# A new order for the prologue of a sketched-attention and expert-routing kernel

## The chip, the cores and the metric

The kernel runs on one core of one Trainium2 chip. A core has a matmul engine (TensorE; PE in the profile, with its weight loads listed as PEld), three engines for elementwise work (VectorE, ScalarE and GpSimd; DVE, ACT and POOL in the profile) and DMA queues, which the SyncE engine (SP) and others issue to. Every engine works through its own instructions in the order of the program, and waits for others by semaphores. Matmul operands lie in SBUF, results land in PSUM, which is divided into banks.

The metric is the device time of the whole program in microseconds, taken as a median over runs. All inputs start in DRAM and the output ends there.

## The reference

Two blocks follow each other. The first is attention with a polynomial sketch instead of a softmax: each row of q and k (32 numbers) is turned into 64 features, the outer product of two projections to 8 numbers.

```python
# q, k, v: (4, 4, 1088, 32) float32; S1, S2: (8, 32), float64
def phi(x):
    a = np.einsum('rd,bhsd->bhsr', S1, x)
    b = np.einsum('rd,bhsd->bhsr', S2, x)
    return np.einsum('bhsi,bhsj->bhsij', a, b).reshape(*x.shape[:-1], 64)
q_p, k_p = (phi(q), phi(k))
kv = np.einsum('bhsf,bhsd->bhfd', k_p, v)
z = np.sum(k_p, axis=2)
num = np.einsum('bhsf,bhfd->bhsd', q_p, kv)
den = np.einsum('bhsf,bhf->bhs', q_p, z)[..., None] + 1e-06
attn_out = (num / den).astype(np.float32)
```

The second block takes the result as 4352 rows of 128 and sends each row to one of 8 experts by a hash of its token number.

```python
x = attn_out.transpose(0, 2, 1, 3).reshape(4352, 128)
expert_idx = token_ids * np.int64(2654435761) % np.int64(8)
for e in range(8):                      # w1: (8, 128, 1024), w2: (8, 1024, 128)
    mask = expert_idx == e
    h = np.maximum(x[mask] @ w1[e], 0.0)
    out[mask] = h @ w2[e]
```

## The kernel before

*Stages.* The program has a prologue, four attention batches and an expert stage. The order of the instructions on each engine is written out by hand; nothing is reordered by a scheduler, so the order of the source is the order of each engine's queue.

*Rows of a batch.* The 1088 rows of a batch are 1024 main rows (8 tiles of 128 partitions, called T, handled as two groups g of Q = 4) and 64 tail rows, which are handled for two batches together. Work on a tile always covers the 4 heads.

*Attention, one batch b.* PE transposes k (`turned`, L458 on) and ACT copies the result to SBUF (`kT`, L470). PE multiplies it with the sketch matrix `s_k`, both projections at once (`k_products`, L499, matmul at L496), which gives 16 numbers per row and head in PSUM. ACT copies all of them to SBUF (`ab`, L511). DVE multiplies the two halves into 64 features (`kp`, L523, two operations per batch, one for each group). PE sums `kv` over the rows (`kv_products`, matmul at L554) from the features and `va`, which is v with a column of ones. For q, DVE makes the transpose (`qT`, L590, and L730 for the first batch), PE the products (`q_products`, `abq_ps`), ACT the copy, DVE the features (`f`, L523) and their transpose (`fT`, L606). ACT cuts the blocks of `kv` that belong to each head into `m` (L576), 16 small copies, whose other entries were zeroed at the start (L229). PE multiplies `fT` with `m` into `x_ps` (L658), ACT copies to `xe` (L661), and DVE (`den`) and GpSimd (`xs`, L686) divide. A store then writes the rows to `x_rows` in DRAM. In the loop each batch also prepares the k and q features of the next one.

*Sketch matrix.* S1 and S2 are 64-bit floats[...]. DVE takes them apart as integers and puts the 32-bit value together (L242 to L266, `s_rep`). One PE transpose and one DVE product with a mask turn this into `s_k` (`s_turned`, L273).

*Routing.* Beside attention, DVE and GpSimd sort the tokens by expert: `route_experts` and `route_scan` count, `route_counts` has three matmuls and an ACT copy (`counts`), `route_bases` finds each expert's place (L323 to L339), `route_order` and `route_ranks` follow, then `route_digits` and `route_slots` on GpSimd and `route_rows`/`route_tiles` on DVE (L416, L426).

*PSUM.* Three pools: `ps` with 4 banks (`bank()`), `ps_x` with 2 (`x_bank`), `ps_o` with 2 (kv sums; later the second layer's sums).

*Loads.* SP issues the loads of all batches (L119), in an order written out at L150 to L161; two tensors of the first batch, and k with them, come in two halves each. ACT's queue brings S2 and the token numbers. The experts' weights follow on SP's queue as soon as the order of the experts is known.

*PE at the start.* Ten matmuls without a result (`keep_busy(WARM)`, L210) run before the first real work, and one more between the k transposes and the first products.

*Expert stage.* Sixteen groups (two for each expert) run through layer 1 (`hp`, L943) and layer 2 (`op`, L951), interleaved. Rows are gathered by GpSimd with indirect DMAs, and result rows are scattered to the output by GpSimd too (L954). GpSimd's queue holds two drains, placed after step 7 of groups 12 and 14 (L1063)[...]. At the end of the stage the last results (`op_rows`, L1140) are copied by ACT (L1142) and scattered.

Of the kernel before, what the change touches and what calls it, by code (L numbers as in the profile page):

```python
# [9 lines left out]
F32 = mybir.dt.float32  # L10
# [20 lines left out]
def kernel(  # L31
# [42 lines left out]
    WARM = 10  # L74
# [25 lines left out]
    nc.scalar.dma_start(tok[:], _words(moe_token_ids).rearrange("(p c two) -> p c two", p=P, two=2))  # L100
# [12 lines left out]
    def load_main(src, b, tag):  # L113
        t = load.tile([P, H, T, D], F32, tag=tag, name=f"{tag}{b}")
        n = parts(b, tag)
        for g in range(n):
            nc.sync.dma_start(t[:, :, g * T // n:(g + 1) * T // n],
                              src[b, :, g * SM // n:(g + 1) * SM // n, :].rearrange("h (p t) d -> p h t d", t=T // n))
        return t  # L119

    def parts(b, tag="q"):

        return 2 if b == 0 else 1
# [25 lines left out]

    act = const.tile([P, 1], F32)  # L150
    nc.scalar.memzero(act[:])
    k_t += [load_main(k, b, "k") for b in range(2)]
    v_t.append(load_main(v, 0, "v"))
    q_t.append(load_main(q, 0, "q"))
    k_tail = load_tail(k, "k_tail")
    v_tail = load_tail(v, "v_tail")
    q_t.append(load_main(q, 1, "q"))
# [70 lines left out]
    for m in ms[0] + ms[1]:  # L228
        nc.scalar.memzero(m[:])  # L229
# [16 lines left out]
    m_hi = shifts("m_hi", hi, 12, 9)  # L246
    nc.vector.tensor_scalar(ex[:], ex[:], 127.0 - 1023.0, 0.0, op0=OP.add, op1=OP.max)
    m_lo = s_tile("m_lo")
    nc.vector.tensor_scalar(m_lo[:], lo, 29, None, op0=OP.logical_shift_right)
    nc.vector.tensor_scalar(ex[:], ex[:], 255.0, None, op0=OP.min)  # L250
    sg = s_tile("sg")
    nc.vector.tensor_scalar(sg[:], hi, 31, 31, op0=OP.logical_shift_right, op1=OP.logical_shift_left)
    live = s_tile("live", F32)
    nc.vector.tensor_scalar(live[:], ex[:], 0.0, None, op0=OP.is_gt)
    nc.vector.tensor_scalar(ex[:], ex[:], 23, None, op0=OP.logical_shift_left)
    rest = shifts("rest", lo, 3, 3)
    nc.vector.tensor_tensor(sg[:], sg[:], ex[:], op=OP.bitwise_or)
    s32 = s_tile("s32", F32)
    nc.vector.tensor_copy(s32[:], rest[:])
    top = s_tile("top")  # L260
    nc.vector.tensor_tensor(top[:], m_hi[:], m_lo[:], op=OP.bitwise_or)
# [193 lines left out]

    x_dram = nc.dram_tensor("x_rows", (N, DM), F32)

    def turned(src, g):  # L458

        p = bank([P, H, P], "kT_ps")  # L460
        for h in range(H):
# [782 lines left out]
```

## Time and profile before

| what | value |
|---|---|
| median of 3 runs | 193.56 us (193.52 to 193.78) |
| profiled execution | 190.24 us |
| its span (first to last recorded instruction) | 188.4 us |
| first kv sum of batches 0, 1, 2, 3 starts | 9.43, 26.94, 39.71, 50.76 us |
| first matmul of the expert stage | 62.33 us |
| end of the last matmul | 183.6 us |

All times inside the program are us from the start of the span. A line of the timeline gives start, duration, engine, source line, operation, output and inputs by the program's names, shapes, the number of instructions it stands for, and in brackets how long the engine was idle before it and what released it. In the table by stage a pair such as "3.93 (x10)" is busy time and number of instructions of one engine.

Some durations that are used below, from the groups by shape up to the start of the expert stage:

| instruction | mean |
|---|---|
| DVE `kp`, 128x1024 (x8) | 1.439 us |
| DVE `f`, 128x1024 (x8) | 1.263 us |
| DVE `fT`, 128x1024 (x8) | 1.246 us |
| DVE `qT`, 128x1024 (x3) / 128x512 (x2) | 1.223 / 0.686 us |
| DVE `kp_tail`, 128x512 | 0.649 us |
| DVE `row` (x2) / `in_tile` / `tiles` | 1.268 / 0.789 / 0.796 us |
| ACT `m` from `kv`, 32x66 (x48) | 0.206 us |
| ACT `xe`, 128x264 | 0.38 us |

### The profile page before, as it was taken

The page shows a single profiled execution, that of the slowest core. Times are in us where ns is not written, and L with a number is a line of the kernel's source. Part 1 is how long each engine was busy: PE and PEld are TensorE (multiplying, and loading weights), DVE is VectorE, ACT ScalarE, POOL GpSimd, SP SyncE. Part 2 cuts the span into 40 slices and gives each one's busy share as a digit, 9 for nine tenths or more (in the row PEclk, how much of TensorE's full clock was granted, in tenths as well). Part 3 has the DMA queues.
Part 4 walks back from the last instruction along what each step waited for, and adds up shares of the span by engine and source line. Part 5 has one row for each costly group of instructions (what it writes and reads, how often), then busy time and mean ns, then how long its engine had stood idle before and what let it go on. Part 6 is the DMA issues. An engine that isn't in the chain of part 4 may idle for free.

```text
span 188.4 us, 3334 instructions
## 1 busy us (share of the span) xinstructions
PE 180.0 (96%) x1066; PEld 154.1 (82%) x1066; DVE 112.3 (60%) x304; ACT 72.9 (39%) x227; POOL 108.1 (57%) x153
## 2 busy tenths in 40 slices
PE   7979999999999999989999999999999999999990
PEld 2869999999998888878888888777777777778990
DVE  5899997999979747455346345345254754424330
ACT  6733783776527432233232232232331323311320
POOL 7258983737482558756766467463664434244573
PEclk9999999999999999999999999999999999999999
DMA  4999999989395721623443343431614243060011
GB/s 125 302 191 294 349 355 342 338 251 339 131 251 153 247 70 44 171 63 84 98 82 77 83 84 66 89 84 42 92 50 95 48 95 69 14 99 28 27 47 36
DMA packets 40115, 25.91 MB, mean 138 GB/s; under 512 B 21236, under 2 KB 37301, under 8 KB 40096
## 3 DMA queue, kind: packets, MB, share of 16 engines
q1 hardware_dynamic: 35152, 18.46, 37.3%
q0 software_dynamic: 2416, 5.08, 10.8%
q10 hardware_dynamic: 2528, 2.13, 4.0%
q8 instruction: 9, 0.15, 0.3%
q14 instruction: 10, 0.08, 0.1%
HBM read 17.41 MB, written 4.52 MB: 116 GB/s over the span
## 4 chain that ended last, share of the span: by engine, by line
PE 72%; DVE 15%; POOL 7%; issue 3%; ACT 1%; POOLq 0%; DVEq 0%
PE hp L943 31%; PE op L951 31%; DVE kp L523 4%; PE kv L554 3%; DVE f L523 3%; PE idle L210 2%; POOL out_dram L954 2%; DVE fT L606 2%; PE ab_ps L496 1%; DVE row L416 1%; PE x_ps L658 1%; PE abq_ps L496 1%; POOL va L541 1%; DVE m L576 1%; POOL over L403 1%
## 5 line engine op out<-in xcount | busy, mean ns | idle before, releaser
L951 PE MATMUL op<-hT,w 128*128 128x256 f32 (+8 forms) x256 | 76.3, 389 | 0.0
L811 DVE TENSOR_SCALAR hT<-hp 128x256 f32<-128x256 f32 (+9 forms) x68 | 29.0, 427 | 54.1 <-PE hp L943 44.8
L954 POOL DMA_INDIRECT out_dram<-os,put x35 | 35.7, 1019 | 38.4 <-DVE os L1012 21.3
L951 PEld LDWEIGHTS op<-hT,w 128*128 128x128 f32 x256 | 47.4, 190 | 10.6
L809 ACT ACTIVATE hT<-hp 128x256 f32<-128x256 f32 (+9 forms) x68 | 26.5, 390 | 64.6 <-PE hp L943 64.1
L803 POOL DMA_INDIRECT xg<-x_rows,idx x33 | 33.9, 1028 | 18.7 <-DVE idx L863 5.6
L943 PE MATMUL hp<-xT_late,w 128*128 128x320 f32 (+8 forms) x144 | 41.9, 386 | 0.0
L943 PE MATMUL hp<-xT,w 128*128 128x256 f32 x128 | 37.1, 380 | 0.5 <-ACT half L991 0.5
L943 PEld LDWEIGHTS hp<-xT_late,w 128*128 128x128 f32 x144 | 25.4, 190 | 6.8
L943 PEld LDWEIGHTS hp<-xT,w 128*128 128x128 f32 x128 | 24.1, 190 | 4.1 <-ACT half L991 0.9
L554 PE MATMUL kv<-va,kp 128*128 128x132 f32 x128 | 15.7, 278 | 0.5 <-DVE kp L523 0.3
L658 PE MATMUL x_ps<-m,fT 128*128 128x132 f32 x128 | 15.7, 279 | 0.1
L554 PEld LDWEIGHTS kv<-va,kp 128*128 128x128 f32 x128 | 14.8, 190 | 0.9 <-issue 0.9
L658 PEld LDWEIGHTS x_ps<-m,fT 128*128 128x128 f32 x128 | 14.9, 190 | 0.4 <-ACT xe L661 0.3
L576 ACT COPY m<-kv 32x66 f32<-32x66 f32 x48 | 9.9, 206 | 7.0 <-PE kv L554 6.4
L686 POOL TENSOR_TENSOR xs<-xe,den 128x512 f32<-128x512 f32 x6 | 7.7, 1302 | 7.7 <-DVE den L681 4.1
L523 DVE TENSOR_TENSOR kp<-ab 128x1024 f32<-128x1024 f32 x8 | 11.2, 1439 | 0.6 <-ACT ab L511 0.6
L1012 DVE COPY os<-turned 128x256 uint16<-128x256 uint16 (+1 forms) x26 | 7.5, 312 | 5.0 <-DMA turned<-half 4.7
L606 DVE STREAM_TRANSPOSE fT<-f 128x1024 f32<-128x1024 f32 x8 | 10.0, 1246 | 0.5
L523 DVE TENSOR_TENSOR f<-ab 128x1024 f32<-128x1024 f32 x8 | 10.1, 1263 | 0.1
L882 DVE COPY xh<-xg 128x256 uint16<-128x256 uint16 (+1 forms) x28 | 9.5, 380 | 0.0
L496 PE MATMUL abq_ps<-s_k,qT 128*128 128x128 f32 (+1 forms) x64 | 7.8, 274 | 1.4 <-DVE qT L730 1.4
(196 smaller groups left out, 175.7 us busy)
## 6 DMA issues: line engine op xcount, KB each, us to landing
w<-in_moe_w_dram SPq DMA_DIRECT2D x12, 512.0 KB, 6.9
w<-in_moe_w_dram ACTq DMA_DIRECT2D x4, 512.0 KB, 5.1
k<-in_k_dram SPq DMA_DIRECT2D x3, 512.0 KB, 7.5
q<-in_q_dram SPq DMA_DIRECT2D x3, 512.0 KB
v<-in_v_dram SPq DMA_DIRECT2D x3, 512.0 KB, 8.6
x_rows<-xs SPq DMA_DIRECT2D x2, 512.0 KB, 3.2
out_dram<-os,put POOLq DMA_INDIRECT x35, 2.3
xg<-x_rows,idx POOLq DMA_INDIRECT x33, 2.6
```

The source lines that it names most:

```text
L496: nc.tensor.matmul(dst, stationary, s.rearrange("p t x r -> p t (x r)").unsqueeze(1).to_broadcast([s.shape[0], n, s.shape[1], 2 * R]), sta ...
L523: eng.tensor_tensor(dst, ab[:, :, 0].unsqueeze(3).to_broadcast(shape), ab[:, :, 1].unsqueeze(2).to_broadcast(shape), op=OP.mult)
L554: nc.tensor.matmul(kv[:].rearrange("p x y -> p (x y)")[:, pr * HA:(pr + 1) * HA], kp[:, t, 2 * pr:2 * pr + 2].rearrange("p h i j -> p (h i ...
L576: copy(m[f][t * D:(t + 1) * D, h::2, t], src)
L606: nc.vector.transpose(fT[:].rearrange("p k (q s) -> p k q s", q=Q), f[:].rearrange("p q h (k d) -> p (h k) q d", d=D))
L658: nc.tensor.matmul(p[:, h], fT[:, (h0 + h) * FB + fb], m[fb][:, h0 + h].rearrange("p t d -> p (t d)"), start=(fb == 0), stop=(fb == FB - 1 ...
L803: nc.gpsimd.indirect_dma_start(out=dst, out_offset=None, in_=x_dram[0:rows], in_offset=bass.IndirectOffsetOnAxis(ap=idx, axis=0), bounds_c ...
L809: nc.scalar.activation(dst, src, AF.Relu if relu else AF.Copy)
L811: return nc.vector.tensor_scalar(dst, src, 0.0, None, op0=OP.max).ins
L943: nc.tensor.matmul(hp[:, 0:hi - lo], w1[:, g % E, c * P:(c + 1) * P], x_columns(first_of(g) + lo, first_of(g) + hi), start=True, stop=True)
L951: nc.tensor.matmul(ops[g][:, 0:hi - lo], w2[:, g % E, c], hTs[g][:, c, lo:hi], start=(c == 0), stop=(c == FC - 1))
L954: st_ = nc.gpsimd.indirect_dma_start(out=out[:], out_offset=bass.IndirectOffsetOnAxis(ap=idx, axis=0), in_=src, in_offset=None, bounds_che ...
```

## The change

The diff touches the prologue and the first turns of the loop, the way features are formed in all batches, two PSUM banks in the last batch, and one drain near the end:

- *Start.* 6 instead of 10 matmuls without a result, and the extra one is gone. The 64-bit to 32-bit conversion has 9 DVE operations instead of 16. Zeroing `m` moves: the first pair to DVE, the second to a later point on ACT.
- *Loads.* k of the first batch comes in four pieces of 128 KB, one of them on ACT's queue, with the token load behind it; v and q of the first batch come whole; q of the second batch is loaded ahead of `v_tail`. The rows of the first batch are stored to `x_rows` with one DMA instead of two.
- *First k.* The sketch's transpose comes first on PE, k is transposed in pairs of heads with an ACT copy each.
- *Features.* ACT copies only the first factor (`first_copied`). DVE reads the second factor from PSUM (`features_of`). The tails keep both factors in SBUF. A products bank is therefore in use until DVE has formed the features; k products are put into `kv_bank`, some others into `x_bank`.
- *Order.* Transposes and products of the second k come ahead of the first kv sum, which then runs in two parts (steps 0 and 1, then all others). `route_bases` is split into `route_places` and the rest, with q's transposes between. In the first turn of the loop the kv tail and the first-factor copy of q come ahead of q's tail products, the tail features ahead of `kp`. `row1`, `in_tile` and `tiles` come after the second `f`.
- *Last batch.* `bring(0)` takes a `kv_bank`, the last x products a `bank`.
- *Drain.* The second drain moves from the end of group 14's step 7 to its step 0.

The core of the diff:

```diff
-    WARM = 10
+    WARM = 6
...
+        for i, eng in enumerate((nc.sync, nc.scalar, nc.sync, nc.sync)):
+            ts, hs = slice(i // 2 * Q, (i // 2 + 1) * Q), slice(i % 2 * 2, (i % 2 + 1) * 2)
+            eng.dma_start(t[:, hs, ts], rows[:, hs, ts])
...
+    k_t.append(load_main(k, 0, "k"))
+    load_tok()
     act = const.tile([P, 1], F32)
     nc.scalar.memzero(act[:])
-    k_t += [load_main(k, b, "k") for b in range(2)]
+    k_t.append(load_main(k, 1, "k"))
     v_t.append(load_main(v, 0, "v"))
     q_t.append(load_main(q, 0, "q"))
     k_tail = load_tail(k, "k_tail")
+    q_t.append(load_main(q, 1, "q"))
     v_tail = load_tail(v, "v_tail")
-    q_t.append(load_main(q, 1, "q"))
...
-    for m in ms[0] + ms[1]:
-        nc.scalar.memzero(m[:])
+    for m in ms[0]:
+        nc.vector.memset(m[:], 0.0)
...
-    m_hi = shifts("m_hi", hi, 12, 9)
-    nc.vector.tensor_scalar(ex[:], ex[:], 127.0 - 1023.0, 0.0, op0=OP.add, op1=OP.max)
...
-    nc.vector.tensor_add(s32[:], s32[:], top[:].bitcast(F32))
+    sign = s_tile("sign")
+    nc.vector.tensor_scalar(sign[:], hi, -(1 << 31), 1 << 30, op0=OP.bitwise_and, op1=OP.bitwise_xor)
+    nc.vector.tensor_scalar(ex[:], ex[:], 1023.0 + 128.0, 1023.0 - 127.0, op0=OP.min, op1=OP.max)
+    high = s_tile("high")
+    nc.vector.tensor_scalar(high[:], hi, (1 << 20) - 1, 1 << 20, op0=OP.bitwise_and, op1=OP.bitwise_or)
+    nc.vector.tensor_scalar(ex[:], ex[:], 24, 1, op0=OP.logical_shift_left, op1=OP.logical_shift_right)
+    low = s_tile("low")
+    nc.vector.tensor_scalar(low[:], lo, 1, None, op0=OP.logical_shift_right)
+    nc.vector.tensor_tensor(ex[:], ex[:], sign[:], op=OP.bitwise_xor)
     s32 = s_tile("s32", F32)
+    nc.vector.scalar_tensor_tensor(s32[:], low[:], 2.0 ** -31, high[:], op0=OP.mult, op1=OP.add)
     s_rep = const.tile([2 * R, Q, D], F32)
+    nc.vector.scalar_tensor_tensor(s_rep[:], s32[:].unsqueeze(1).to_broadcast([2 * R, Q, D]), 2.0 ** -20,
+                                   ex[:].bitcast(F32).unsqueeze(1).to_broadcast([2 * R, Q, D]), op0=OP.mult, op1=OP.mult)
...
+    def pair_turned(kT, src, g, pr):
+        hs = slice(2 * pr, 2 * pr + 2)
+        nc.scalar.copy(kT[:, hs], turned(src, g, range(H)[hs])[:])
...
+    def first_copied(ab_ps):
+
+        n = ab_ps.shape[1] * H * Q
+        a = work.tile([P, n, R], F32, tag="first", name="first_of_ab", bufs=3)
+        nc.scalar.copy(a[:], ab_ps[:].rearrange("p g t h y -> p (g t h) y")[:, :, 0:R])
+        return a, ab_ps[:].rearrange("p g t h y -> p (g t h) y")
+
+    def features_of(dst, ab, g):
+
+        a, ps_ = ab
+        r = slice(g * H * Q, (g + 1) * H * Q)
+        shape = [P, H * Q, R, R]
+        nc.vector.tensor_tensor(dst, a[:, r].unsqueeze(3).to_broadcast(shape),
+                                ps_[:, r, R:2 * R].unsqueeze(2).to_broadcast(shape), op=OP.mult)
...
+    kTs = [kT_tile() for _ in range(GQ)]
+    s_turned(x_bank)
+    pair_turned(kTs[0], k_t[0], 0, 0)
+    pair_turned(kTs[0], k_t[0], 0, 1)
+    pair_turned(kTs[1], k_t[0], Q, 0)
     route_experts()
-    kTs = [transposed(k_t[0], 0)]
-    s_turned()
-    kTs.append(transposed(k_t[0], Q))
-    keep_busy(1)
     route_scan()
     va = values(v_t[0], T, work, "", None)
-    abk = ab_tile()
     kp = work.tile([P, T, H, R, R], F32, tag="kp", name="kp", bufs=1)
-    parts_ps = [k_products(kTs[g:g + 1]) for g in range(GQ)]
-    copy_ab(abk, parts_ps[0], 0, src=0)
+    abks = [first_copied(k_products(kTs[0:1], kv_bank))]
     nc.scalar.copy(cp[:], seq[:, :, C - 1])
-    copy_ab(abk, parts_ps[1], Q, src=0)
-    k_features_of(kp, abk, 0, Q)
+    pair_turned(kTs[1], k_t[0], Q, 1)
+    abks.append(first_copied(k_products(kTs[1:2], x_bank)))
+    for g in range(GQ):
+        k_features_main(kp, abks[g], g, 0)
+    kTs = [transposed(k_t[1], g) for g in range(0, T, Q)]
     cnt = route_counts()
+    abk_ps = k_products(kTs, kv_bank)
     for g in range(GQ):
         ts = slice(g * Q, (g + 1) * Q)
         nc.scalar.copy(va[:, ts, :, 0:D], v_t[0][:, :, ts].rearrange("p h t d -> p t h d"))
-    kTs = [transposed(k_t[1], g) for g in range(0, T, Q)]
-    kv = kv_products(0, (kp, va), (kp_tail, va_tails), None, upto=Q)
-    k_features_of(kp, abk, Q, T)
-    route_bases(cnt)
+    abk = first_copied(abk_ps)
+    route_places(cnt)
     route_order()
...
+    kv = kv_products(0, (kp, va), (kp_tail, va_tails), None, upto=2)
     kTt = k_tail_turned()
+    abqs = [first_copied(q_products(qT[:, :, 0:Q], Q, x_bank))]
+    abt = k_tail_products(kTt)
+    abqs.append(first_copied(q_products(qT[:, :, Q:T], Q, x_bank)))
+    route_bases(cnt)
+    for m in ms[1]:
+        nc.scalar.memzero(m[:])
     digits = route_ranks()
     route_order_end()
...
-    kv = kv_products(0, (kp, va), (kp_tail, va_tails), kv, Q + 2)
     route_digits(digits)
-    abt = k_tail_products(kTt)
-    abk_ps = k_products(kTs)
     kv = kv_products(0, (kp, va), (kp_tail, va_tails), kv, T)
-    abk = copied(abk_ps)
-    fTs = [q_features(abq, 0)]
     k_features_of(kp_tail, abt, 0, TT)
     qT = q_blocks(q_t[1], T)
     qT_tail = q_tail_blocks()
-    fTs.append(q_features(abq, 1))
+    fTs = [q_features(abqs[0], 0, 0)]
+    fTs.append(q_features(abqs[1], 1, 0))
...
         m = kv_diagonal(b, kv)
         if b == 0:
-            tail = q_tail_copied(abt_ps)
+            m_tail = kv_tail(b, kv)
+            abq = first_copied(abq_ps)
+            tail = q_tail_copied(q_tail_products(qT_tail))
             kT_ps = [turned(k_t[b + 2], g) for g in range(0, T, Q)]
+            fT_tail = q_tail_features(tail)
         else:
-            abk = copied(abk_ps)
+            abk = first_copied(abk_ps)
         kp = k_features(abk, T, work, "")
...
-    bring(0)
-    x_products(e, 1, fTs[1], last_m)
+    bring(0, kv_bank)
+    x_products(e, 1, fTs[1], last_m, bank)
...
-        if g in (G - 4, G - 2):
+        if g == G - 4:
 
             at(g, 7, nc.gpsimd.drain)
+        if g == G - 3:
+            at(g + 1, 0, nc.gpsimd.drain)
```

## The prediction

> **What bounds the kernel now.** I read the busy table and the chain first, then busy time by stage, then the timeline around each stage's border.
>
> ```profile
> PE 180.0 (96%) x1066; PEld 154.1 (82%) x1066; DVE 112.3 (60%) x304; ACT 72.9 (39%) x227; POOL 108.1 (57%) x153
> ...
> PE 72%; DVE 15%; POOL 7%; issue 3%; ACT 1%; POOLq 0%; DVEq 0%
> ```
>
> The matmul engine (PE) is busy 96% and carries 72% of the chain, so only idle PE and the ends can give time. Borders for the stages: last dummy matmul, first q product, second and fourth kv sum, first MoE layer, last matmul. Columns: busy time of PE, PEld, DVE, ACT, POOL, then clock, DMA share, GB/s.
>
> ```profile
> 0.00:4.90 4.90, 3.93 (x10) 1.49 (x11) 2.90 (x20) 3.04 (x6) 3.66 (x27) 1.00 0.48 130
> 4.90:12.83 7.93, 6.34 (x54) 5.65 (x53) 6.94 (x18) 4.89 (x12) 2.37 (x10) 1.00 1.04 235
> 12.83:26.94 14.11, 14.11 (x127) 13.91 (x127) 13.70 (x17) 8.48 (x35) 12.41 (x25) 1.00 1.07 332
> 26.94:50.76 23.82, 23.54 (x232) 23.16 (x231) 22.06 (x27) 15.57 (x58) 13.42 (x17) 1.00 0.95 295
> 50.76:62.33 11.57, 11.25 (x95) 10.46 (x95) 9.91 (x22) 5.41 (x20) 5.75 (x5) 1.00 0.70 197
> 62.33:183.60 121.27, 120.79 (x555) 99.47 (x553) 56.75 (x204) 35.21 (x100) 68.85 (x70) 1.00 0.35 76
> ```
>
> From 12.83 on PE idles 14.11-14.11 = 0, then 0.28, 0.32 and 0.48. The gaps are in the first 12.83 us, where the first 4.90 hold dummy work alone. So PE work must start earlier, or fill the 1.59 idle of the second row (1.36 of it one wait, below). DVE is nearly as full (13.70 of 14.11): the next bound.
>
> ```profile
> 4.87 0.28 DVE L266 TENSOR_TENSOR s_rep<-s,live 16x128 f32<-16x128 f32 x1
> ...
> 7.76 2.36 DVE L523 TENSOR_TENSOR kp<-ab 128x1024 f32<-128x1024 f32 x2 [0.57 <-ACT ab L511]
> ...
> 12.83 1.97 PE L496 MATMUL abq_ps<-s_k,qT 128*128 128x128 f32 x16 [1.36 <-DVE qT L730]
> ...
> 36.21 4.10 DVE L523 TENSOR_TENSOR kp<-ab 128x1024 f32<-128x1024 f32 x2
> ```
>
> The sketch matrix is ready at 5.15, k features end at 10.12, PE waits for q's transpose; and one pair of features takes 4.10 at 36.21, not 2.36.
>
> The end:
>
> ```profile
> 170.91 0.98 POOL L954 DMA_INDIRECT out_dram<-os,put  x1 [3.87 <-DVE os L1012]
> 172.20 0.98 POOL L954 DMA_INDIRECT out_dram<-os,put  x1 [0.30 <-issue]
> 175.57 0.98 POOL L954 DMA_INDIRECT out_dram<-os,put  x1 [2.38 <-issue]
> ...
> 184.57 0.98 POOL L954 DMA_INDIRECT out_dram<-os,put  x1 [0.30 <-ACTq L1152]
> ...
> 183.65 0.27 ACT L1142 COPY os<-op_rows 128x128 f32<-128x128 f32 x1 [1.92 <-PE op_rows L1140]
> ...
> L1063 POOLq DRAIN  x2: 3489/5200/6910, 155.8 to 171.2; - x2
> ```
>
> The second drain (171.2, 3.49 us) holds the scatters until 175.57. From there they follow every 1.285 us, and the last starts 0.65 after its data (183.65+0.27 = 183.92).
>
> [...] dummy matmuls come every 0.43 us, and every 0.22 from about 4.7, 3.7 after the first. [...] the 4.10 lies beside GpSimd's `xs` (34.01 to 38.2), and beside DVE's pair at 21.56 a small GpSimd operation takes 1.19 (L391) instead of 0.26 (L393). [...] The trace shows no surcharge: 64 elements take 0.225 with a PSUM input (`s_k`) and 0.224 without (L330).
>
> **The change part by part.**
>
> *Start.* Sixteen conversion operations become nine (2.47 to 5.15 is 0.168 each; nine at 0.15 to 0.17 end at 3.9). Turn and `s_k` follow in 0.9 as before (5.15 to 6.02): `s_k` at 4.8, 1.2 sooner. k's first batch in four 128 KB pieces: halves landed at 3.88 and 4.67; two rings carry them now, the pieces usable by 4.2 to 5.3 with the extra packets, so k and `s_k` meet. Eight products take 0.9, so the first `ab` is done at 6.1 (7.3 before). The shortened ACT copy (0.27) ends at 6.5, but routing's scan, ahead on DVE, ends about 6.9. First features 6.9 to 8.1, second by 9.6 (10.12 before). `m` zeroing moves from ACT to DVE's idle 0.96: nothing. Tokens queue behind one k piece on ACT's queue, needed by about 5: nothing, 0.3 if late. v's 512 KB in one DMA still lands about 8.1. q1 ahead of `v_tail` delays the latter from 12.45 to about 14.2; GpSimd's copies then end at 15.2, before kv(0)'s tail wants them: nothing.
>
> *Second k's products ahead of kv.* Their 1.95 us and transposes (1.07) fill PE's idle 1.59, but the two `kT` copies (1.06) now stand on ACT before `counts`, moving it from 8.70 to about 9.9, and with it DVE's routing. kv(0)'s first part (8 matmuls) runs 11.0 to 11.9, q's products from 11.9 instead of 12.83; then tail products 0.5, second q half 0.97, 24 + 4 kv matmuls 3.3: kv(0) ends about 17.2 (19.51 before).
>
> *DVE between there and kv(1).* From 9.9, with before's durations: routing 1.15 (places) + 1.30 (two qT) + 0.87 (bases) + 1.07 (ranks) + 0.20 (order), `kp_tail` 0.65, qT 1.22, qT_tail 0.67, two f and fT pairs 4×1.22 = 4.88, f_tail and its transpose 1.51, first half of kp(1) 1.22: sum 14.74, ending at 24.64. One wait goes in: f_tail needs ACT's `tail`, now behind 16 `m` copies (3.49), the kv tail (0.5) and an `abq` copy: 17.2+0.2+3.49+0.5+0.4+1.12 = 22.9, against DVE there at 21.9. I take 0.7 of the 1.0, since ACT's operations overlap a little (one starts at 8.25 for 0.37, the next at 8.52); behind it wait kp(1) and then PE. kv(1) starts at 25.3. PE itself would be ready at 17.2+(26.94-19.51) = 24.6. So gain 26.94-25.3 = 1.65, and DVE is now what comes last.
>
> *Steady stages.* PE has 0.28 idle to 50.76 and 0.32 beyond: of these 0.60 I take 0.3, since features no longer collide with GpSimd (4.10 to 2.45, f at 45.55 from 1.68 to 1.2; DVE falls from 22.06 to about 20 of 23.8). ACT copies half as many elements: off the path. The features hold their PSUM bank until DVE is done, 1 to 3 us longer; the main kv sums have two banks alternating with k products, each released by features before the next but one: cost 0, at most 0.3 a batch, 0.9 in all. `row1` and `tiles` (2.86 us of DVE) behind the second f: their list is read after kv(2), 10 us later: nothing. One x_rows store instead of two: batch 0's rows are gathered after 51: nothing. Swapped banks in the last batch: 0 to 0.1.
>
> *PSUM as a source.* 13 feature operations up to kv(3)'s start: 0 by the 0.225 to 0.224 pair[...].[...] I take 0.
>
> *Tail.* The drain moves to the gap between the scatter ending 167.04 and 170.91. A drain here lasted up to 6.91, so it may end at 168.5 to 172; even from 172 the ten scatters left, 1.285 apart, put the last at 172+9×1.285 = 183.6, before its data (183.9). The last scatter starts at 183.97, not 184.57: gain 0.60. SP isn't passed.
>
> *Sum.* 1.65 + 0.3 + 0.6 = 2.55. The span goes from 188.4 to 185.85, the profiled execution from 190.24 to 187.7. The median of the runs, 193.56, stands 3.3 above that execution; I let the 3.3 stand: 191.0.
>
> **The rivals.**
> - *The clock stays half longer.* Six dummies end at 3.5 instead of 5.1, and PE then has gaps[...]. The first eight products then take 1.8, all after them 0.9 later: kv(1) at 26.2, gain 0.75+0.3+0.6 = 1.65: 191.9. For it: 6×0.43 = 2.6 of activity is less than 3.7. Against: transposes follow from 4.
> - *DVE's chain eats the prologue.* [...] only the tail is left: 193.0. For it: DVE 13.70 of 14.11. Against: PE's order has slack.
> - *More than that:* PE fed without the wait, and the whole 0.6: gain 1.65+0.7+0.6+0.6 = 3.55, 190.0.
> - *Slower: reading PSUM drags each DVE feature operation.* Place: `kp` and `f`, where PE writes and ACT reads other PSUM banks meanwhile. If each costs p more, kv(1) moves by 5p-1.65, the middle stage by 8p-3.9 once that is above 0 (23.8-20 of DVE slack), the last by p, less the tail's 0.6. From p = 0.44 the whole is a loss (6p = 2.65 before the middle stage tells). The only price for a dragged operation here is (4.10-2.45)/2 = 0.83: 2.5+2.7+0.8-0.6 = 5.4, so 199.0. For it: no large PSUM×SBUF operation is in the trace. Against: the `s_k` pair, and DVE's `hT` from PSUM, 0.423 for 256 and 0.492 for 320 elements: 1.08 ns each[...], as for 1024 from SBUF (1.22).
>
> **How the numbers follow.** Forecast 0.58, clock 0.19, DVE chain 0.10, more 0.04, PSUM price 0.09. A measurement of this kernel tells about 0.2% (0.39 us) from no change. Of the DVE chain's 0.10, 0.04 lies within that: faster 0.58+0.19+0.06+0.04 = 0.87, same 0.04, slower 0.09. The range: below, half the way beyond "more" (189.5); above, the clock case with 0.9 for banks held longer (192.8). Outside: the PSUM price, half of the DVE chain, a part of "more": 0.09+0.06+0.02 = 0.17.
>
> **What would show it.** Right: `s_rep` ending near 3.9; first `kp` before 7.2; kv(1) at 25.3 with DVE as releaser; `kp` at 1.22 each, also beside `xs`; layer 1 at 60.4, its stage unchanged at 121.3; the last scatter right behind its data. Wrong: dummy-rate matmuls at half speed beyond 6; `kp` over 1.5; a wait of kv on `m` copies or of products on a bank; a late drain. Any change in the MoE stage other than the drain would make the sum wrong.

## The result and the profile after

The changed kernel takes 191.46 us (median of 6, 191.07 to 192.32), the kernel before 193.67 in the same comparison (median of 6). The ratio is 0.9875, with a 95% interval of 0.9831 to 0.9919. The forecast was 191.0. Two more comparisons of the unchanged pair gave 0.9942 (0.9920 to 0.9965; 190.23 against 190.96 us) and 0.9899 (0.9860 to 0.9938; 192.06 against 193.90 us). Medians and ratios leave out runs more than 1.5% above the fastest of the same kernel. So it is faster in all three, by 0.7 to 2.2 us at the medians. The parts of the forecast are another matter, and most of this section and the next is about them.

The profiled execution of the changed kernel took 192.06 us with a span of 190.3. That of the kernel before, shown ahead of the prediction, took 190.24 with a span of 188.4. The single profile of before was thus a quick execution (its runs lie at 193.5), and the two spans cannot simply be subtracted. Places inside the two programs can be.

Busy time by stage of the changed kernel, with the borders at the same events as in the table before (first work after the matmuls without result, first q product, second and fourth kv sum, first layer-1 matmul, last matmul). The columns are as there: PE, PEld, DVE, ACT, POOL, clock, DMA share, GB/s.

```profile
0.00:4.00 4.00, 2.74 (x6) 0.74 (x7) 2.80 (x15) 1.49 (x2) 2.94 (x19) 1.00 0.33 97
4.00:13.17 9.17, 8.16 (x61) 7.36 (x62) 6.54 (x14) 4.57 (x13) 2.80 (x18) 1.00 1.02 269
13.17:26.94 13.77, 13.36 (x119) 12.97 (x118) 12.02 (x18) 8.53 (x34) 10.60 (x31) 1.00 1.00 305
26.94:50.48 23.54, 23.49 (x231) 23.11 (x231) 23.02 (x29) 14.24 (x54) 6.97 (x11) 1.00 0.97 304
50.48:61.94 11.46, 11.03 (x95) 10.44 (x95) 9.79 (x22) 5.56 (x20) 5.29 (x5) 1.00 0.70 199
61.94:184.69 122.75, 120.98 (x555) 99.49 (x553) 56.68 (x204) 35.06 (x100) 68.99 (x70) 1.00 0.31 75
```

The second kv sum begins at 26.94, as before; the forecast had 25.3. From there to layer 1 the two stages shrank from 23.82 to 23.54 and from 11.57 to 11.46, 0.39 together (0.30 forecast). GpSimd's busy time in the middle stage fell from 13.42 to 6.97: about 3.1 of it is seven small operations of `route_slots` and what follows it, which now lie ahead of kv(1), and about 3.5 is shorter divisions (8.36 to 4.89). The expert stage is 1.48 longer than before (122.75 against 121.27).

The timeline of the changed kernel, at the places that the prediction named:

```profile
3.60 0.28 DVE L261 SCALAR_TENSOR_TENSOR s_rep<-s,ex 16x128 f32<-16x128 f32 x1
...
8.71 1.07 PE L458 MATMUL kT_ps<-ident,k 128*128 128x128 f32 x8 [0.34 <-DMA k<-in_k_dram]
...
24.25 0.69 DVE L659 TENSOR_TENSOR f<-ab_tail 128x512 f32<-128x512 f32 x1 [1.41 <-ACT ab_tail L651]
...
24.55 2.07 PE L671 MATMUL x_ps<-m,fT 128*128 128x132 f32 x16 [0.41 <-ACT xe L674]
...
34.30 2.40 DVE L412 TENSOR_TENSOR row<-number,st 128x2176 bf16<-128x2176 bf16 x1
...
38.15 2.35 DVE L531 TENSOR_TENSOR kp<-first_of_ab,ab_ps 128x1024 f32<-128x1024 f32 x2
```

The sketch matrix is done at 3.88 (forecast 3.9). The transposes of the second k begin at 8.71 after a wait for their load (8.0 follows from the prediction's sum: 11.0 less 1.95 and 1.07). The pair of features that took 4.10 now takes 2.35. But GpSimd is idle beside it (from 35.54 to 43.56), so this pair says nothing about the new source. It is `row`, moved behind the second f, that now lies beside GpSimd's work (the tail's division up to 34.49, a copy of `va` from 34.51 to 35.54), and it takes 2.40 instead of 1.27.

The end of the program, ACT, PE and GpSimd:

```profile
180.77 0.28 ACT L1002 COPY late_cols<-op 128x143 f32<-128x143 f32 x1 [3.39 <-PE hp L952]
...
181.19 0.41 PE L1028 MATMUL tp<-ident,late_cols 128*128 128x128 f32 x2 [1.28 <-ACT late_cols L1002]
...
185.09 0.27 ACT L1153 COPY os<-op_rows 128x128 f32<-128x128 f32 x1 [2.28 <-PE op_rows L1151]
185.63 0.98 POOL L963 DMA_INDIRECT out_dram<-os,put  x1 [1.15 <-ACT os L1153]
```

PE has a wait of 1.28 here that the profile of before does not have; it makes up nearly all of the 1.48. The last scatter is no longer queued behind others: it follows its data (185.36) by 0.27.

### The profile page after: what moved, and what is told of

It is laid out like the page before. It is cut to its first block, busy times and chain, and to the rows that moved or that the text cites. A ratio compares the mean times of both kernels' runs of the same rounds, so it can differ in the third digit from the quotient of the medians.

```text
span 190.3 us, 3310 instructions
## 1 busy us (share of the span) xinstructions
PE 179.8 (94%) x1061; PEld 154.1 (81%) x1061; DVE 110.9 (58%) x299; ACT 69.7 (37%) x221; POOL 98.6 (52%) x153
## 5 line engine op out<-in xcount | busy, mean ns | idle before, releaser
L699 POOL TENSOR_TENSOR xs<-xe,den 128x512 f32<-128x512 f32 x6 | 6.2, 1049 | 13.1 <-DVE den L694 13.1
L531 DVE TENSOR_TENSOR kp<-first_of_ab,ab_ps 128x1024 f32<-128x1024 f32 x8 | 9.4, 1208 | 0.4 <-ACT first_of_ab L523 0.4
L531 DVE TENSOR_TENSOR f<-first_of_ab,abq_ps 128x1024 f32<-128x1024 f32 x8 | 9.5, 1193 | 0.2
L499 PE MATMUL ab_ps<-s_k,kT 128*128 128x128 f32 (+1 forms) x64 | 8.2, 277 | 0.6 <-ACT kT L474 0.4
```

Source lines behind the costliest of these rows:

```text
L531: nc.vector.tensor_tensor(dst, a[:, r].unsqueeze(3).to_broadcast(shape), ps_[:, r, R:2 * R].unsqueeze(2).to_broadcast(shape), op=OP.mult)
```

## The experiments

All are variants of the changed kernel or of the kernel before, timed beside the kernel before. There were three comparisons, each with its own executions of the kernel before (medians 190.96, 190.79 and 193.90 us): the first has the four kernels of the next table, the second has `warm8`, both factors in SBUF, k in two halves and the later products, the third has the last four. The second has no execution of the changed kernel itself, so its kernels can be set against the changed kernel only by their ratios to the kernel before.

### The two kernels again, and the drain alone

Edits: none for the first two. The third puts the drain of the changed kernel back, the fourth moves it in the kernel before:

```diff
-        if g == G - 4:
-            at(g, 7, nc.gpsimd.drain)
-        if g == G - 3:
-            at(g + 1, 0, nc.gpsimd.drain)
+        if g in (G - 4, G - 2):
+            at(g, 7, nc.gpsimd.drain)
```

> The kernel before, unchanged. The profile shown before the prediction (span 188.4, execution 190.24) is 3.3 us under the median of the runs. Theory A, that execution was an unusual one: this profile's span comes near 191.5, and the extra 3 us lie in one or two places (a stall of one engine) that can be named. Theory B, the profile is typical and the timed runs carry a constant extra: span near 188.4 with a time near 190.

> The changed kernel, unchanged. In its first profile the second kv sum starts at 26.94, as before, and the last part has PE idle for 1.28 us before the last out_rows. If the prologue's gain was really nothing, kv(1) again starts at 26.9 and layer 1 near 61.9; if it was one execution's accident, kv(1) starts near 25.3. If the stall at the end is chance, it is gone or in another place here. Time 191.0 to 192.

> The changed kernel with the second drain back behind step 7 of group 14. Prediction's theory: the last scatters queue again, 0.6 us slower than the changed kernel (about 192.0). Rival: the drain is worth all of the 2.4 us that was measured, then 193.5. Second rival: the drain was not what the end waited for, no difference.

> The kernel before with the second drain moved to step 0 of group 14 and nothing else. Prediction's theory: 0.6 us faster than before (193.0). Rival, that the drain carries the whole gain: 191.4.

| kernel | median us | ratio to before (95%) | kv(1) starts | layer 1 starts |
|---|---|---|---|---|
| before again | 191.02 | 1.0008 (0.9985 to 1.0031) | 26.73 | 61.98 |
| changed again | 190.23 | 0.9942 (0.9920 to 0.9965) | 27.95 | 62.82 |
| changed, drain back | 190.23 | 0.9967 (0.9948 to 0.9987) | 25.81 | 60.97 |
| before, drain moved | 190.78 | 1.0010 (0.9986 to 1.0034) | 27.62 | 63.06 |

The expected times were all too high, since this comparison as a whole ran 2.7 us quicker than the one with the result (190.96 instead of 193.67 for the kernel before). The span of the kernel before did come near 191.5 (191.3), with 3 us in two places that are shown in the last section, but its execution took 193.1 against a median of 191.0: here the profiled execution was the unusual one.

The drain. Moved in the kernel before it gives nothing, and put back in the changed kernel it leaves the median where it was (190.23 both; the intervals of the ratios overlap). The two profiles of the kernel before, with the drain in its old place (upper) and moved (lower), show why 0.6 was too much:

```profile
186.41 0.27 ACT L1142 COPY os<-op_rows 128x128 f32<-128x128 f32 x1 [1.92 <-PE op_rows L1140]
187.07 0.98 POOL L954 DMA_INDIRECT out_dram<-os,put  x1 [0.31 <-ACTq L1152]
```

```profile
184.40 0.27 ACT L1144 COPY os<-op_rows 128x128 f32<-128x128 f32 x1 [1.92 <-PE op_rows L1142]
184.94 0.98 POOL L954 DMA_INDIRECT out_dram<-os,put  x1 [0.79 <-ACT os L1144]
```

With the queue the last scatter starts 0.39 after its data (187.07-186.68), without it 0.27 (184.94-184.67): 0.12 us. With nothing ahead of it the last scatter still started 0.27 after its data (in this profile and in the changed kernel's first), which the prediction had as 0.05, and how far the queue reaches past the data differs from execution to execution (0.65 in the first profile, 0.39 here).

The prologue. The three profiles of the same prologue put kv(1) at 26.94, 27.95 and 25.81: it varies by 2 us from execution to execution. The good one first, then the bad one:

```profile
7.79 1.04 PE L458 MATMUL kT_ps<-ident,k 128*128 128x128 f32 x8
...
25.81 0.37 PE L570 MATMUL kv<-va,kp 128*128 128x132 f32 x1
```

```profile
5.88 1.81 PE L499 MATMUL ab_ps<-s_k,kT 128*128 128x128 f32 x8
...
9.51 1.48 PE L458 MATMUL kT_ps<-ident,k 128*128 128x128 f32 x8
...
27.95 1.27 PE L570 MATMUL kv<-va,kp 128*128 128x132 f32 x9
```

In the bad one the products come at a slower pace (1.81 for eight, against 1.10 in the other two); the clock records of that trace show the full clock from 10.4 only, against 5.06 (first) and 4.66 (good). That is the prediction's clock rival, in one execution of three. In all three, kv(1) starts 18.0 to 18.4 after the second k's transposes (25.81-7.79, 26.94-8.71, 27.95-9.51), so most of what differs between executions is decided ahead of those transposes.

### Two more matmuls without result

```diff
-    WARM = 6
+    WARM = 8
```

> The changed kernel with 8 matmuls without a result instead of 6. In one of three profiles of the changed prologue the first products came at half pace (1.81 us for 8 instead of 1.10) and batch 1's kv sum started at 27.95 instead of 25.81. Theory: the two extra ones fill PE's gap between 3.7 and 4.4, and the clock is then full when k arrives: no half-pace products, kv(1) at 26.0, and 0.3 to 0.8 us faster than the changed kernel at the median. Rival: [...] PE's queue is held 0.4 longer: 0 to 0.4 slower.

190.01 us, ratio 0.9955 (0.9934 to 0.9976); the profile has the full clock from 3.79, the first eight products in 1.10, and kv(1) at 26.29. The matmuls without result begin at 0.97 in every profile, so the full clock came 2.8 after the first of them here and 9.4 after it in the bad profile above: the 3.7 that the prediction read from one trace is no fixed measure. Set against the changed kernel's 0.9942, of another comparison, no difference is shown. The theory's 0.3 to 0.8 is not seen at the median; whether the slow pace (1.81) is too rare or costs too little to move it is not shown. The eight profiles with six such matmuls have the full clock from 4.2 to 10.4, two of them after 8 (10.4, and 8.02 with the later products); the other six, with eight or ten, from 3.8 to 6.6.

### Both factors in SBUF

```diff
-        a = work.tile([P, n, R], F32, tag="first", name="first_of_ab", bufs=3)
-        nc.scalar.copy(a[:], ab_ps[:].rearrange("p g t h y -> p (g t h) y")[:, :, 0:R])
-        return a, ab_ps[:].rearrange("p g t h y -> p (g t h) y")
+        a = work.tile([P, n, 2 * R], F32, tag=f"first{n}", name="first_of_ab", bufs=2)
+        nc.scalar.copy(a[:], ab_ps[:].rearrange("p g t h y -> p (g t h) y"))
+        return a, a
```

(The features then read the first factor from the same tile; the tail's `ab_tile` for q shares the smaller of the two tags.)

> The changed kernel with both factors copied to SBUF by ScalarE, so that DVE reads no PSUM for k and q features. Prediction's theory: the kp pair beside GpSimd's xs goes back from 2.35 to about 4.1 and f to 1.7, kp elsewhere stays at 1.2; PE had 0.3 us from it, so 0.2 to 0.5 slower than the changed kernel. Rival: features from PSUM cost something of their own (longer bank holding), then this is as fast or faster. Second rival: the feature change carries the gain of the whole, then it falls back to the time of the kernel before.

191.28 us, ratio 1.0024 (1.0003 to 1.0044): no faster than the kernel before, and by the interval a little slower. The new order without the new features loses all of the gain, as the second rival had it. Its timeline, PE, DVE and GpSimd:

```profile
35.72 2.03 DVE L412 TENSOR_TENSOR in_tile<-number,st 128x1224 bf16<-128x1224 bf16 x1
...
38.49 2.35 DVE L531 TENSOR_TENSOR kp<-first_of_ab 128x1024 f32<-128x1024 f32 x2
...
39.86 3.84 PE L570 MATMUL kv<-va,kp 128*128 128x132 f32 x32 [0.37 <-DVE kp L531]
...
43.92 2.75 POOL L699 TENSOR_TENSOR xs<-xe,den 128x512 f32<-128x512 f32 x2 [6.83 <-DVE den L694]
...
46.08 1.68 DVE L531 TENSOR_TENSOR f<-first_of_ab 128x1024 f32<-128x1024 f32 x1
...
51.30 1.93 PE L570 MATMUL kv<-va,kp 128*128 128x132 f32 x15 [0.60 <-DVE kp L531]
```

And the changed kernel at the place of `xs` and `f`:

```profile
43.56 2.05 POOL L699 TENSOR_TENSOR xs<-xe,den 128x512 f32<-128x512 f32 x2 [8.02 <-DVE den L694]
45.58 0.39 POOL L710 TENSOR_TENSOR xs_tail<-xe,den 64x128 f32<-64x128 f32 x1
...
45.73 1.22 DVE L531 TENSOR_TENSOR f<-first_of_ab,abq_ps 128x1024 f32<-128x1024 f32 x1
```

The operations of DVE and GpSimd that lie beside each other slow down again (`xs` 2.75 for two, 2.05 with features from PSUM; `f` 1.68 instead of 1.22), DVE falls behind, and PE waits for `kp` at the third and fourth kv sum. One part of the expectation missed: the `kp` pair does not go back to 4.1, it stays at 2.35 with both factors in SBUF, because the moved `row`, `in_tile` and `tiles` now take its place beside GpSimd. The slower division (2.84 for the first pair, 2.06 in the changed kernel) reaches further into these three: from the start of `row` to `kp` they take 4.48 instead of 3.85, 0.63 more, and the slower `f` adds 0.46. DVE itself has no wait between 25.30 and 52.2, so neither ScalarE's longer copies nor the fewer buffers of this edit held it there. Busy time from kv(1) to layer 1, both factors in SBUF, then the changed kernel, then the kernel before:

```profile
26.63:62.82 36.19, 34.76 (x325) 33.55 (x324) 34.07 (x50) 20.67 (x73) 20.47 (x23) 1.00 0.84 259
```

```profile
26.94:61.94 35.00, 34.52 (x326) 33.55 (x325) 32.81 (x50) 19.81 (x73) 12.27 (x16) 1.00 0.88 270
```

```profile
26.94:62.33 35.39, 34.80 (x327) 33.63 (x325) 31.97 (x48) 20.98 (x77) 19.17 (x22) 1.00 0.87 263
```

The features from PSUM take 36.19-35.00 = 1.19 out of these stages, of which the profile shows 0.97 as the two waits for `kp`. Against before there remains 0.39, since the new order puts more of DVE's work here (32.81 busy, 31.97 before, despite the shorter features).

### The features alone

In the kernel before, with everything else as it was (loads, order, conversion, drain), the first factor is copied, the second read from PSUM, and the products' banks are taken as in the changed kernel:

```diff
-    parts_ps = [k_products(kTs[g:g + 1]) for g in range(GQ)]
-    copy_ab(abk, parts_ps[0], 0, src=0)
+    parts_ps = [k_products(kTs[g:g + 1], (kv_bank, x_bank)[g]) for g in range(GQ)]
+    abks = [first_copied(parts_ps[0])]
...
-    k_features_of(kp, abk, Q, T)
+    k_features_main(kp, abks[1], 1, 0)
...
-            abk_ps = k_products(kTs)
+            abk_ps = k_products(kTs, kv_bank)
```

> The kernel before with the feature change alone: ScalarE copies one factor, DVE reads the other from PSUM, banks as in the changed kernel; prologue, loads and drain as before. With both factors in SBUF the changed kernel lost all its gain (1.0024). Theory now: features from PSUM are the larger part, because the stages from the second kv sum to layer 1 get shorter by 0.3 to 0.4 and the chain of DVE no longer meets GpSimd: ratio 0.995 to 0.998. Rival, the prediction's weights: the feature change alone gives 0.3 us (0.9985) and the rest comes from the prologue's order. Second rival: it is worth something only with the new order, alone nothing (1.000 or more).

> The changed kernel unchanged, on the chip of the three kernels below, as their measure. Expected ratio to before 0.993 to 0.996, as in the last comparison (0.9942).

193.46 us, ratio 0.9962 (0.9933 to 0.9991), where the changed kernel in the same comparison has 0.9899 (0.9860 to 0.9938). The way from kv(1) to layer 1 is the shortest of the profiles compared here (first fence), and DVE now waits for its input (second fence; GpSimd is idle beside this pair). The `f` at 43.38 lies wholly beside GpSimd's division (43.23 to 45.28) and takes 1.22, the division 2.05:

```profile
27.53:62.26 34.73, 34.29 (x326) 33.48 (x325) 29.10 (x47) 19.79 (x73) 13.12 (x19) 1.00 0.88 266
```

```profile
35.80 2.35 DVE L528 TENSOR_TENSOR kp<-first_of_ab,ab_ps 128x1024 f32<-128x1024 f32 x2 [1.28 <-ACT first_of_ab L520]
...
43.38 1.22 DVE L528 TENSOR_TENSOR f<-first_of_ab,abq_ps 128x1024 f32<-128x1024 f32 x1
```

So the feature change alone is worth about 0.7 us by the ratio (0.0038 of 194; 0.2 to 1.3 by the interval), 0.66 by its stage in this one profile (35.39-34.73). The prediction had 0.3 for it. Why the whole kernel does better still in this comparison (1.2 us more by the ratio, though the intervals overlap) the profiles do not say: layer 1 starts at 62.26 in this one and at 62.34 in the changed kernel's of the same comparison.

### k in two halves, and the second k's products later

The first edit loads k of the first batch in two DMAs from SyncE; the second puts the second k's transposes behind the counts and its products behind the first steps of kv(0):

```diff
-        for i, eng in enumerate((nc.sync, nc.scalar, nc.sync, nc.sync)):
-            ts, hs = slice(i // 2 * Q, (i // 2 + 1) * Q), slice(i % 2 * 2, (i % 2 + 1) * 2)
-            eng.dma_start(t[:, hs, ts], rows[:, hs, ts])
+        for ts in (slice(0, Q), slice(Q, T)):
+            nc.sync.dma_start(t[:, :, ts], rows[:, :, ts])
```

```diff
-    kTs = [transposed(k_t[1], g) for g in range(0, T, Q)]
     cnt = route_counts()
-    abk_ps = k_products(kTs, kv_bank)
...
-    abk = first_copied(abk_ps)
+    kTs = [transposed(k_t[1], g) for g in range(0, T, Q)]
...
     kv = kv_products(0, (kp, va), (kp_tail, va_tails), None, upto=2)
+    abk_ps = k_products(kTs, kv_bank)
+    abk = first_copied(abk_ps)
```

> The changed kernel with k of the first batch in two halves of 256 KB on SyncE's queue, instead of four pieces on two queues. In the changed kernel the last k piece landed at 5.3 to 5.9 (4.7 to 5.2 before). Theory: the pieces bring the first transposes forward (4.2 instead of 4.9) and are worth 0.2 to 0.5 us. Rival: the late end of the pieces costs as much as their early start brings: no difference.

> The changed kernel with the second k's transposes behind the counts, and its products behind the first two steps of kv(0). Prediction's theory: the early products fill PE's idle time and are worth about 1 us of the prologue, so kv(1) is 0.7 to 1.2 later than in the changed kernel, and the kernel loses most of its gain. Rival: what PE gains there it loses by routing's counts coming later (10.4 instead of 8.5): no difference, kv(1) the same.

Halves: 190.58 us, ratio 0.9973 (0.9952 to 0.9993), kv(1) at 27.26. Later products: 190.27 us, ratio 0.9974 (0.9953 to 0.9995), kv(1) at 26.91. Each is 0.003 above the changed kernel's 0.9942 of the first comparison, about 0.6 us, with intervals that overlap: each may be worth some tenths, and neither is shown to be worth anything. The later products did not lose "most of the gain". Their profile is of interest:

```profile
9.15 1.07 PE L458 MATMUL kT_ps<-ident,k 128*128 128x128 f32 x8
...
26.91 1.27 PE L570 MATMUL kv<-va,kp 128*128 128x132 f32 x9
```

kv(1) comes 17.76 after the transposes, no later than with the early products (18.0 to 18.4), and this although its full clock came at 8.02 only and its first eight products took 1.81: in this one profile the two orders come to the same, as the rival of this run had it.

### The second k in halves, and a mix

```diff
+        if (b, tag) == (1, "k"):
+            for ts in (slice(0, Q), slice(Q, T)):
+                nc.sync.dma_start(t[:, :, ts], rows[:, :, ts])
+            return t
```

The mix adds WARM = 8 and, in the loop's first turn (batch 0), a free bank for the first x products of the second group.

> The changed kernel with the second batch's k loaded in two halves of 256 KB, so that the first four of its transposes need only the first half. In two profiles PE waited for this load until 8.7; in the good one it began at 7.8, and everything up to kv(1) follows at fixed distances. Theory: the landing of the second k (with the completion seen 1.2 to 1.5 us after the last packet) is what the prologue lost, so the transposes begin by 8.0, kv(1) at 26.0 or less and the time is 0.3 to 0.7 under the changed kernel's. Rival: PE is held by the first k's products and copies just as long, or one more DMA delays the others: no difference or slower.

> The changed kernel with the second k in two halves, 8 matmuls without a result, and the first x products of batch 0's second group in a free bank, since PE idles 0.41 us there for a ScalarE copy in all profiles of the changed kernel. Theory: these add up, kv(1) 0.4 earlier than with the split alone, 0.5 to 1.2 us under the changed kernel. Rival: DVE's kp(1), which is formed just ahead of kv(1), then comes last, and the wait for the copy is replaced by one for kp: no more than the split alone.

Split: 191.95 us, ratio 0.9907 (0.9870 to 0.9945). Mix: 191.63 us, ratio 0.9900 (0.9856 to 0.9943). The changed kernel beside them: 192.06 us and 0.9899. PE's transposes of the second k in the unchanged kernel of this comparison, in the split and in the mix, and kv(1) of the mix:

```profile
9.11 1.06 PE L458 MATMUL kT_ps<-ident,k 128*128 128x128 f32 x8 [1.15 <-DMA k<-in_k_dram]
```

```profile
8.04 1.05 PE L462 MATMUL kT_ps<-ident,k 128*128 128x128 f32 x8
```

```profile
8.55 1.05 PE L462 MATMUL kT_ps<-ident,k 128*128 128x128 f32 x8
...
26.55 1.70 PE L574 MATMUL kv<-va,kp 128*128 128x132 f32 x13 [0.23 <-DVE kp L535]
```

The split takes the wait for the load away, and kv(1) comes at 26.51 instead of 27.18 in these profiles (26.0 or less was expected); the time does not follow beyond the noise. In the mix the 0.41 wait for `xe` is gone, and PE waits for DVE's `kp` instead, as its rival said. No version was shown to beat the changed kernel.

## Why the prediction was right in total and wrong in its parts

The total. Forecast 2.55 us; measured 2.2, 0.7 and 1.8 at the medians of three comparisons. The direction was right, and the time in the comparison with the result lies 0.46 above the forecast. That it lies so near is in good part luck: the parts that the profiles place add up to 0.3 to 0.5, the largest part of the forecast is not there, and the 3.3 between the profiled execution of before and its median, which the prediction carried over to the changed kernel, did not recur (192.06 against a median of 191.46). Of the rivals, the slower one (a price for reading PSUM) fell at once, since `kp` takes 1.21 and `f` 1.19 on average, like the quick ones of before (median of `kp` 1.22, `f` 1.16 to 1.22; by its own terms it would have become a loss from p = 0.43, not 0.44). The clock rival is real in some executions (1.81 for the first eight products in two of the eight profiles with six matmuls without result, where it expected 1.8). The rival that DVE's chain eats the prologue has the size right, but the time is lost earlier.

*Prologue, 1.65 at kv(1): measured about nothing.* kv(1) starts at 25.81, 26.94, 27.18 and 27.95 in the four profiles with this prologue unaltered (median 27.06), and at 26.73, 26.94 and 27.62 in three of the kernel before with its own (median 26.94). The prediction's way to kv(1) has four stretches. The columns are the changed kernel with the drain back, in its first profile, in the third comparison and again:

| stretch | forecast | drain back | first | third | again |
|---|---|---|---|---|---|
| start of the second k's transposes | 8.0 | 7.79 | 8.71 | 9.11 | 9.51 |
| from there to q's first products | 3.9 | 4.35 | 4.57 | 4.41 | 4.78 |
| from there to the end of kv(0) | 5.3 | 5.55 | 5.55 | 5.54 | 5.55 |
| from there to kv(1) | 8.1 | 8.12 | 8.11 | 8.12 | 8.11 |

The first three were too short. The first, because the load was seen late (waits of 0.34 and 1.15) or the full clock came late (10.4). The step of the prediction that overlooked this is "k's first batch in four 128 KB pieces": it followed the pieces of the first k and not the load behind them, whose last packet came at 7.19 in the first profile, while PE began at 8.71. In the second, the products wait 0.24 for ScalarE's `kT` copies, the counts' matmuls go ahead of them, and the tail's two transposes, 0.2 of PE's time, stand ahead of q's first products. The third is a slip in the sum: 0.97, 0.5, 0.97 and 3.3 from 11.9 give 17.64 as the end of kv(0), not 17.2. With it the forecast for kv(1) is 25.7, and the best of the four profiles has 25.81.

*"DVE is now what comes last": right, and the fourth stretch with it.* The lines of PE show no wait at kv(1), but their ends are modelled, and the end of DVE's first `kp` operation tells more. In PE's recorded waits for `kp` (the two in the kernel with both factors in SBUF, the one of the mix, and 0.28 at the fourth kv sum before) the kv sum starts 0.15 after `kp` ends. With the new order kv(1) starts 0.15 after it in every profile; in the kernel before it is 4.2. The changed kernel first, then the mix, then the kernel before:

```profile
24.11 0.67 ACT L674 COPY xe<-x_ps 128x264 f32<-128x264 f32 x2
...
25.61 1.18 DVE L531 TENSOR_TENSOR kp<-first_of_ab,ab_ps 128x1024 f32<-128x1024 f32 x1
...
26.94 0.37 PE L570 MATMUL kv<-va,kp 128*128 128x132 f32 x1
```

```profile
25.22 1.18 DVE L535 TENSOR_TENSOR kp<-first_of_ab,ab_ps 128x1024 f32<-128x1024 f32 x1
```

```profile
24.08 0.39 ACT L661 COPY xe<-x_ps 128x264 f32<-128x264 f32 x1
...
21.56 2.38 DVE L523 TENSOR_TENSOR kp<-ab 128x1024 f32<-128x1024 f32 x2
```

DVE's wait for `tail` (1.41 in the first profile, 0.7 was taken) is part of this stretch. PE's own chain is ready at most 0.1 sooner (kv(1) starts 0.39 to 0.46 after the tail's x products, against 0.38 in the kernel before), since its x products waited 0.41 for `xe`. Both hang on ScalarE, where the new order puts the kv tail and the copy of q's first factor (0.43 and 0.37) ahead of `tail` and `xe`: from the end of kv(0) to `xe` it takes 5.28 instead of 4.57, and to kv(1) 8.11 instead of 7.43. So the new order gives back 0.7 here. The prediction had these 0.7 in its sum (25.3 against 24.6 for PE alone), for DVE only. In the mix PE no longer waits for `xe`, and kv(1) still comes 8.10 after kv(0). To put the two copies behind `xe` again was not tried.

*Steady stages, 0.3: measured 0.39 in the first pair, and mis-sized as a cause.* From kv(1) to layer 1 three profiles of the kernel before take 35.25 to 35.44, four of the changed kernel's order and features 34.87 to 35.16. Features from PSUM are worth about 0.7 us alone and 1.2 to 1.6 inside the new order (1.19 by the stage; 0.0082 of 191 by the ratios, across two comparisons). That they would keep to about 1.2 beside GpSimd was the author's estimate: the trace of before shows only what both factors in SBUF took there (4.10 for the pair, 1.68 for one `f`), and the runs then bore it out (`f` 1.16 to 1.22). The prediction bounded their worth by PE's idle time before; it did not ask what the moved `row1`, `in_tile` and `tiles` would do to DVE if the features stayed slow. Its cost of nothing for them, because their list is read late, looked at who needs them and not at what stands behind them on DVE: `row` itself became 1.13 longer, and all of them push `kp`. And the 4.10 that it wanted to save was only in part beside the division: the main rows' ends at 36.85 and the tail's at 38.18, then comes the copy of `va` to 39.23. In the new order the pair meets none of these, whatever its source.

*Tail, 0.6: measured 0.1 in the profiles, and none in the times.* The term that was mis-sized is the start of the last scatter after its data: 0.27, not 0.05. The queue before was longer than its data by 0.65 only in the profile at hand.

*What the profiles leave open.* They place some 0.3 to 0.5 us of the gain; the medians show 0.7 to 2.2. With a start that varies by 2 us between executions, single profiles cannot place the rest. Nor is it known why the kernel before loses more than the changed one in the comparison with the result and in the last one (2.7 and 2.9 us above its 191.0, the changed one 1.2 and 1.8 above its 190.2): no profile of the kernel before was taken there. The clocks on record give a small part of it. In the last comparison 5 of 23 executions of the kernel before and 11 of 21 with the features alone have a mean granted clock of 0.983 to 0.987, and none of 22 with the new order. Without these, the medians are 193.6 and 193.0, and the changed kernel's 192.1. Whether the order has to do with it is not shown: one execution with the later products has 0.985 as well.

## What to carry to other kernels

When a change moves work between engines, cost the moved operations together with the ones that they push, under both settings of every other part of the change; here the new order without the features was no faster than before (1.0024), and the features made it pay (0.9875 to 0.9942). Where a prologue is fed by loads, follow the second one too (PE waited 0.34 and 1.15 for it here), and since one profile gives one draw (kv(1) at 25.81 to 27.95), look at several before a forecast of a microsecond. Where an engine's record shows no idle time, as PE's at kv(1), compare the start of its work with the end of what it reads (0.15 here) before calling it free of the other engine. Measure the start of an operation after its data on an unqueued one (0.27 for the last scatter) before counting a queue as lost time.

## What the runs showed of the hardware

With one input from PSUM, DVE's `f` took 1.16 to 1.22 beside GpSimd's division, as alone (in the changed kernel and with the features alone). With both inputs in SBUF one `f` in each of four profiles took 1.67 to 1.68 (at 45.55 in the kernel before, at 46.08 with both factors in SBUF), but the one at 43.07 in the kernel before, 0.31 ahead of the division at 43.38, took 1.16 there as well. GpSimd gained too: two divisions 2.05 instead of 2.75 to 2.84, its tail's division 0.39 instead of 1.37. `row`, with both inputs in SBUF, took 2.40 beside GpSimd's copy of `va`, and 1.25 to 1.29 alone. No price for the PSUM source was visible in 1024-element operations (`kp` 1.21 on average, against a median of 1.22 from SBUF).

The full clock came between 3.8 and 10.4 us after the start of the span. Both starts after 8 had six matmuls without result, but fourteen profiles are too few to tell whether their number matters. In the second profile of the kernel before, the granted clock was 0.50 for 3.41 us in the middle of the expert stage as well. What stands ahead of it, and the stretch itself by stage:

```profile
81.63 0.67 PE L943 MATMUL hp<-xT,w 128*128 128x256 f32 x2 [1.90 <-issue]
...
81.02 0.51 DVE L888 COPY xT<-xh_turned 128x256 uint16<-128x256 uint16 x2 [2.98 <-DMA xh_turned<-xh]
```

```profile
82.64:86.05 3.41, 3.41 (x10) 2.70 (x9) 1.54 (x7) 0.47 (x2) 2.24 (x3) 0.50 0.29 58
```

A DMA transpose was late there: DVE waited 2.98 for it, and PE, whose next matmul reads the `xT` that DVE then made, stood idle for 1.90 (1.4 to 1.5 and 0.5 at the same place in the other profiles). The clock of 0.50 began 1.0 after PE's idle time had ended (82.64-81.63). In that execution layer 1 to the last matmul takes 124.4 instead of 121.3: an estimate is 1.4 for the wait (1.90-0.5) and 1.7 for the clock (half of 3.41). Whether the wait brought the lower clock about is not shown.

Near the end, the wait of 1.25 to 1.9 us that the changed kernel's profile shows at 181.19 was in all five profiles taken with the result and in the last comparison, with the drain in either place (1.89 with the old place, in the one profile that has it; 1.25 to 1.29 with the new one), and in none of the nine others. ACT and DVE saw PE's sums late at the same moment. Its cause was not found.
